# All two-tile attention groups of batches 2 to 4 turned by DMA transpose, and a list planner's durations replaced by measured ones

## The chip, the cores and the metric

The kernel runs on one core of one Trainium2 chip. The metric is the device time of one execution in microseconds (us). A core has five engines with an instruction queue each: PE (matmul), DVE (vector), ACT (activation), POOL (GpSimd) and SP, which here only issues DMAs. Each engine issues its own queue in order.

## The reference

Three layers follow one another, all in float32:

```
scores = q @ k^T / 8                          # 4 batches, 8 heads, 576 x 576, head size 64
keep   = scores >= rowmax(scores) - tau       # tau = 0.02
p      = softmax(scores where keep else -1e9)
x      = (p @ v), heads joined                # 2304 tokens x 512
y      = square(relu(x @ w_in)) @ w_out       # 512 -> 2048 -> 512
logits = y @ phi                              # 32 slots
slot_in  = softmax over tokens(logits)^T @ y
slot_out = relu(slot_in @ w1[e]) @ w2[e]      # 8 experts, 4 slots each
out    = softmax over slots(logits) @ slot_out
```

The second layer's weights arrive as float64 and are converted on the chip.

## The kernel before, in words

**Work.** A *pair* is two heads of one batch: 4 pairs per batch, 16 in all. A pair has five query tiles: four of 128 rows by both heads (in the code `j` 0 to 3), made into two *groups* (`g` 0 and 1) of two tiles, and one mixed tile of the last 64 rows of both heads (`g` 2). One tile is: scores on PE (`s_mm`, L471 to L482, one PSUM buffer); per head on DVE the clipped negative scores with their row extreme (`top`, L498), on POOL the bound extreme + tau (`bound`, L504), on ACT the exponential (`expo`, L510), on DVE the masking with its row sum (`keep`, L514).

**Two ways to turn the probabilities.** For the product with V they are needed transposed. *PE path*: nine 128x128 transposes per tile (`turn`, through the helper at L241), copied out of PSUM by ACT (`evac`, L579 and L577), then a float32 product with V (`av`, L627 and L616). *DMA path*: ACT makes a half-precision copy (`high`, L532), POOL the rest e - high, also in half precision (`low`, L536), both into a tile `hl` (two buffers), which SP turns with one DMA transpose (`dturn`, L543); then `av_split` (L635, L640) multiplies high by the high and low halves of V and low by the high half. The halves of V are made once per pair by `split_v` (into the only buffer `vh`), in every pair that has a group on this path. `by_dma(p, g)` decides: batch 1 and all mixed tiles go by PE; of batches 2 to 4 the second group of every pair, and the first group of the second and fourth pair. After either, row sums are inverted (`recip`, L599), spread, turned and multiplied in (`evac`, L657 or L659) into `xp`.

**Feed-forward.** Tokens go in nine units of 256 (two per batch, one of all remainders). A unit splits x into two parts (`xhi` L897, `xlo` L903), runs 16 blocks of 12 matmuls (`mm_half`, L932; the plan's `f_a` and `f_b`), squares on ACT and DVE, and then does the softmax step over slots and the accumulation of the slot inputs (`post`). A unit of a batch can only start when the batch's attention is done. The weight conversion (`conv_ops`) must be done before the first unit. `weights` and `tail` load w1 and w2 into buffers freed by attention and by the last unit, and finish.

**Order.** Nothing is ordered by hand. Every step is handed to `Plan` (`add`) with its engine, a modelled duration, its inputs, buffers it takes and gives back, and a key. `Plan.run` plays a clock: a free engine starts, among the steps whose inputs are ready and whose buffers are free, that of the lowest key, and emits its instructions then. That fixes each engine's queue for good; on the chip an instruction waits its turn even if a later one could run. Attention has low keys; feed-forward on PE has keys from 1e5 up, so that it fills what attention leaves. `LEAD` shifts keys by kind. A DMA is modelled on one bus: it starts 1.13 us after issue or when the bus is free, takes its `dma` time, and is seen 0.95 us after; a negative `dma` (the transpose) also holds SP until 0.95 us before the bus is free. SP issues nothing when the bus is booked more than 2.212 us ahead.

Of the kernel before, what the change touches and what calls it, by code (L numbers as in the profile page):

```python
# [139 lines left out]
def tile_kernel(  # L140
# [115 lines left out]
    def conv_ops():  # L256
# [10 lines left out]
        def chunk(n, w, r0, c0):  # L267
# [41 lines left out]
            a = add("c_scale", "ACT", 0.53, scale, [l], k, ["cv"])  # L309
            t = add("c_low", on, 0.53 if on == "ACT" else 0.35, low, [l], k)  # L310
            s = add("c_shift", "DVE", 0.61, shift, [a, t], k)
            if flip:
                s = [s, add("c_unit", "ACT", 0.53, unit, [a], k)]
                s = add("c_flip", "POOL", 1.25, sign, s, k, rel=[("raw64", l)])
            else:
                s = add("c_sign", "DVE", 0.61, sign, [s], k, rel=[("raw64", l)])
            if w is w_in:
                hi, lo = [w_sb[x, c0 // CW][:, r0 // 128, :] for x in ("h", "l")]
                h = add("c_hi", "ACT", 0.53, lambda: nc.scalar.activation(hi, o["p"], AF.Copy), [s], k)
                return add("c_lo", "POOL", 1.23, lambda: nc.gpsimd.tensor_tensor(lo, o["p"], hi.bitcast(F32), ALU.subtract),  # L320
                           [h], k, rel=[("cv", a)])
# [18 lines left out]
            g = add("c_turn", "PE", 0.6, turn, [s], k, ["mm", "wt"])  # L340
# [3 lines left out]
            pr = add("c_prod", "PE", 1.05, prod, [e, lphi], k, rel=[("wt", g)])  # L344
# [8 lines left out]
    def attn_ops():  # L353
# [56 lines left out]
        def split_v(x):  # L410
# [39 lines left out]
            sc = add("v_scale", "DVE", 0.5, scales, [st], k0, rel=[("mm", st)])  # L450
# [4 lines left out]
        def tiles(p):  # L455
# [5 lines left out]
            def tile_ops(n, j):  # L461
# [23 lines left out]
                S_ = add("s", "PE", 1.4, s_mm, d["ready"], k, ["s"])  # L485
# [3 lines left out]
                for a in heads:  # L489
# [92 lines left out]
                for x in heads + (2,):  # L582
# [3 lines left out]
                    t = add("turn", "PE", 0.13 if x == 2 else 0.49, lambda x=x: turn(x), dep + [gd.get("pto")], k, ["mm"] + new, [(tag, ee)])  # L586
                    v_ = add("p_evac", "ACT", 0.27 if x == 2 else 0.59, lambda x=x: evac(x), [t], k, [], [("mm", t)])
# [3 lines left out]
            def group_ops(g, n):  # L591
# [16 lines left out]
                rc = add("recip", "DVE", 0.5, recip, gd["keep"], k, ["rp"], [("sm", gd["first"])])  # L608
# [52 lines left out]
                if g < 2:  # L661
                    rc = add("spread", "POOL", 0.6, spread, [rc], k, ["rb"], [("rp", rc)])
# [13 lines left out]
                rt = add("r_turn", "PE", 0.13 if g == 2 else 0.26, rturn, [rc], k, ["mm", "rr"], rel)  # L676
                rc = add("r_evac", "ACT", 0.3 if g == 2 else 0.4, revac, [rt], k, [], [("mm", rt)])
                deps = gd["turn"] + [d["v_op"], d["vr_op"]]
                first = None
                if by_dma(p, g):  # L680
                    o = first = add("av", "PE", 1.9, av_split, deps + [d["vs_ready"]], k, ["ma"],
                                    [("pt", gd["pto"]), ("vh", d["vs_op"])])
                for lo, hi_ in () if by_dma(p, g) else ((0, 5),) if g == 2 else ((0, 2), (2, 5)):
                    c = (hi_ - lo) * (0.51 if g < 2 else 0.3) 
# [7 lines left out]
                ev = add("evac", "DVE", 0.25 if g == 2 else 0.45, evac, [o, rc], k, ["xp"] if g < 2 and kk == 0 else [], rel)  # L692
# [34 lines left out]
    def ffn_ops(units):  # L727
# [9 lines left out]
        def post(u, d, first, last):  # L737
# [77 lines left out]
            a0 = add("f_pl", "PE", 1.53, lambda: pl(0, MC // NG - 1), d["sq"][:-2], pk(), ["mm"])  # L815
            a = add("f_pm", "PE", 0.51, lambda: pl(MC // NG - 1, MC // NG), [a0] + d["sq"][-2:], pk())
            a2 = add("f_l4", "ACT", 0.26, lambda: nc.scalar.activation(l4, w["pl"][:, :NU], AF.Copy), [a], HI, ["l4"], [("mm", a0)])
            b_ = add("f_p12", "PE", 0.43, p12, [a2], pk(), ["mm"])
            bk = add("f_p1k", "PE", 0.35, p1k, [b_], pk(), [], [("l4", a2)])
            c = add("f_max", "DVE", 0.45, rowmax, [b_, fo.get("nm")], HI)  # L820
            e = add("f_alpha", "ACT", 0.5, alpha, [c, fo.get("nm")], HI, ["dT"], [("mm", b_)])
            f = add("f_total", "DVE", 0.12, total, [e, fo.get("ss")], HI)
            g = add("f_cmax", "DVE", 0.39, cmax, [bk], HI + 1)
            h = add("f_ce", "ACT", 0.15, lambda: nc.scalar.activation(w["ce"], w["ce"], AF.Exp), [g], HI + 1)
            add("f_csum", "DVE", 0.80, csum, [h], HI + 1, rel=[("mm", b_)])
            i_ = add("f_p3", "PE", 0.25, p3, [e], pk(), ["mm"], [("dT", e)])
            j_ = add("f_dk", "DVE", 0.2, dkc, [i_], HI, rel=[("mm", i_)])
            lastsg, turns = fo.get("sg"), []
            for t in range(T):
                gks, ro = [], []  # L830
                for j in range(NG):
# [23 lines left out]
                    ro.append(add("f_gk", "DVE" if dv else "ACT", 0.6 if dv else 0.49, evac, [tt], HI + 2, rel=[("mm", tt)]))  # L855
# [21 lines left out]
                for t_, (accum, merge, ro, gks) in enumerate(turns):  # L877
                    joint = last and t_
                    ac = add("f_acc", "PE", 0.93, accum, ro + [j_] + ([ac0] if joint else []), pk(), [] if joint else ["mm"], gks)
# [8 lines left out]
        for n, u in enumerate(units):  # L888
# [17 lines left out]
            for kk in range(KC):  # L906
# [3 lines left out]
                l = add("xlo", "DVE" if dv else "POOL", 0.35 if dv else 0.69, lambda f=xlo, kk=kk: f(kk), [h] + ls[:1],  # L910
# [332 lines left out]
```

## Time and profile before

| | us |
|---|---|
| three runs, lowest, median, highest | 695.98, 696.82, 704.65 |
| profiled execution, first to last instruction (span) | 694.8 |
| PE busy | 630.1 |
| DVE busy | 456.8 |
| ACT busy | 393.2 |
| POOL busy | 233.1 |

The page gives the profiled execution no time beside its span. Busy times are sums over the whole run, which has stages with different limits: weight conversion with batch 1 (to 155.7 us), attention of batches 2 to 4 with feed-forward units between (to 523.2 us), feed-forward alone (to 618.2 us), and the experts with the output. "PEld" is the loading of PE's stationary operand, "PEclk" the granted clock of TensorE as a share of its full speed.

### The profile page before, as it was taken

How to read it: one execution, taken by the hardware profiler on the slowest of the kernel's cores; microseconds unless marked ns; L12 is line 12 of the kernel's file. 1: busy time of each engine (PE TensorE's matmuls, PEld its weight loads, DVE VectorE, ACT ScalarE, POOL GpSimd, SP SyncE). 2: the span in 40 equal slices, each digit the busy share in tenths (PEclk: the TensorE clock that was granted, in tenths of full speed). 3: DMA queues.
4: the chain of work that ended last, by engine and by line, in shares of the span. 5: the costliest groups of instructions: out<-in, count | busy, mean ns of one | idle time of the engine just before them, and what ended most of it. 6: DMA issues, size and time to landing. Idle time of an engine off the chain costs nothing.

```text
span 694.8 us, 13413 instructions
## 1 busy us (share of the span) xinstructions
PE 630.1 (91%) x5084; PEld 458.4 (66%) x5084; DVE 456.8 (66%) x1183; ACT 393.2 (57%) x762; POOL 233.1 (34%) x308
## 2 busy tenths in 40 slices
PE   1566988999999999999999999999999999998883
PEld 0333656677857686677778667877788989883321
DVE  6999998975787868777966797778733132222503
ACT  4776756766765764766667557757653333331203
POOL 4866433212643434354244344344440000000000
PEclk9987999999999999999999999999999999999998
DMA  6854676422633545163437235352533940397987
GB/s 230 296 180 150 202 246 220 147 93 52 122 70 87 122 70 116 40 135 66 91 73 117 56 69 123 69 122 53 86 59 119 401 174 31 124 371 267 388 321 272
DMA packets 123056, 104.74 MB, mean 151 GB/s; under 512 B 90736, under 2 KB 95856, under 8 KB 122992
## 3 DMA queue, kind: packets, MB, share of 16 engines
q1 hardware_dynamic: 122992, 103.89, 52.0%
q8 instruction: 40, 0.66, 0.4%
q14 instruction: 24, 0.20, 0.1%
HBM read 73.73 MB, written 8.91 MB: 119 GB/s over the span
## 4 chain that ended last, share of the span: by engine, by line
PE 74%; DVE 10%; DMA 5%; ACT 4%; issue 4%; POOL 1%; SPq 0%; DVEq 0%; POOLq 0%; ACTq 0%
PE mm L932 30%; PE mm L241 11%; PE s L482 8%; PE po L627 4%; DVE e L514 3%; PE po L635 3%; PE mm L861 2%; PE mm L747 2%; PE mm L1063 2%; DMA w<-in_moe_w_dram 2%; PE s L477 2%; DMA w_out<-cv 2%; PE s L471 2%; DVE cv L293 2%; ACT e L510 1%
## 5 line engine op out<-in xcount | busy, mean ns | idle before, releaser
L932 PE MATMUL mm<-xh,w 128*128 128x256 f32 x1152 | 167.1, 288 | 0.0
L932 PEld LDWEIGHTS mm<-xh,w 128*128 128x128 f32 x1152 | 147.4, 191 | 16.7 <-issue 10.5
L514 DVE SCALAR_TENSOR_TENSOR e<-u,sm,e 128x576 f32<-128x576 f32 x144 | 125.4, 885 | 26.1 <-ACT e L510 22.9
L498 DVE TENSOR_SCALAR_CACHE_REDUCE u<-s,nscale 128x576 f32<-128x576 f32 x144 | 115.3, 811 | 26.0 <-PE s L482 20.5
L510 ACT ACTIVATE e<-u,sm 128x576 f32<-128x576 f32 x144 | 109.3, 775 | 38.7 <-DVE u L498 36.4
L536 POOL TENSOR_TENSOR hl<-e,hl 128x576 f16<-128x576 f32 x72 | 95.5, 1337 | 84.6 <-ACT hl L532 69.9
L504 POOL TENSOR_SCALAR sm<-sm,tau_p 128x1 f32<-128x1 f32 x144 | 60.7, 424 | 141.1 <-DVE u L498 108.9
L932 PE MATMUL mm<-xl,w 128*128 128x256 f32 x576 | 92.4, 283 | 0.0
L938 ACT ACTIVATE gt<-mm 128x512 f32<-128x512 f32 x72 | 42.9, 596 | 83.3 <-PE mm L932 82.8
L932 PEld LDWEIGHTS mm<-xl,w 128*128 128x128 f32 x576 | 79.3, 192 | 0.0
L482 PE MATMUL s<-kt,qt 64*128 64x512 f32 x256 | 77.0, 680 | 0.0
L241 PE MATMUL mm<-ident_r,e 128*128 128x128 f32 (+1 forms) x332 | 53.3, 296 | 6.0 <-DVE e L514 5.2
L241 PEld LDWEIGHTS mm<-ident_r,e 128*128 128x128 f32 (+1 forms) x332 | 39.9, 151 | 26.8 <-issue 10.0
L477 PE MATMUL s<-kt,qt 128*128 128x128 f32 x128 | 27.2, 295 | 31.0 <-DMA qt<-in_q_dram 11.8
L532 ACT ACTIVATE hl<-e 128x576 f16<-128x576 f32 x72 | 48.1, 679 | 11.8 <-DVE e L514 11.5
L579 ACT ACTIVATE pt<-mm 128x512 f32<-128x512 f32 x72 | 41.7, 594 | 21.9 <-PE mm L241 21.6
L944 DVE SCALAR_TENSOR_TENSOR gt<-mm,gt 128x512 f32<-128x512 f32 x18 | 12.4, 690 | 61.1 <-ACT gt L938 60.3
L477 PEld LDWEIGHTS s<-kt,qt 128*128 128x128 f32 x128 | 20.8, 199 | 36.1 <-issue 19.7
L627 PE MATMUL po<-pt,raw 128*64 128x64 f32 (+1 forms) x480 | 42.0, 309 | 0.0
L241 PE MATMUL mm<-ident_r,gt 128*128 128x128 f32 x288 | 38.3, 278 | 1.4 <-DVE ar L813 1.4
L241 PEld LDWEIGHTS mm<-ident_r,gt 128*128 128x128 f32 x288 | 31.5, 142 | 12.1 <-issue 8.2
L946 ACT ACTIVATE gt<-gt 128x512 f32<-128x512 f32 x54 | 33.9, 627 | 1.1
(148 smaller groups left out, 889.4 us busy)
## 6 DMA issues: line engine op xcount, KB each, us to landing
w<-in_moe_w_dram SPq DMA_DIRECT2D x25, 1024.0 KB, 11.9
raw<-in_moe_w_in_dram SPq DMA_DIRECT2D x16, 512.0 KB, 4.3
raw<-in_moe_w_out_dram SPq DMA_DIRECT2D x16, 512.0 KB, 4.0
kt<-in_k_dram SPq DMA_DIRECT2D x20, 320.0 KB, 3.3
qt<-in_q_dram SPq DMA_DIRECT2D x20, 320.0 KB, 3.7
raw<-in_v_dram SPq DMA_DIRECT2D x20, 256.0 KB, 3.1
w_out<-cv SPq DMA_DIRECT2D x16, 256.0 KB, 4.7
w<-w_out SPq DMA_DIRECT2D x4, 1024.0 KB, 9.1
```

The costliest lines, as they stand in the source:

```text
L241: nc.tensor.transpose(out_, in_, ident[:n, :n])
L477: nc.tensor.matmul(s[:, 1].rearrange("p (c s) -> p c s", s=64)[:, 0:8:7], lt, d["kt"][:, 512:SQ], start=True, stop=True)
L482: nc.tensor.matmul(s[:, 2 * a], lt[i], d["kt"][i, 0:512], start=True, stop=True)
L498: nc.vector.tensor_scalar(u, o["s"][:, s0:s0 + S], nscale, None, ALU.mult, ALU.min, accum_out=gd["sm"][:, c:c + 1])
L504: nc.gpsimd.tensor_scalar(sm[:, 4 + c:5 + c], sm[:, c:c + 1], tau_p, None, ALU.add)
L510: nc.scalar.activation(e, o["u", a], AF.Exp, scale=-1.0, bias=gd["sm"][:, c:c + 1])
L514: nc.vector.scalar_tensor_tensor(e, o["u", a], sm[:, 4 + c:5 + c], e, ALU.is_le, ALU.mult, accum_out=sm[:, 8 + c:9 + c])
L532: nc.scalar.activation(o["hl"][:, a * S:(a + 1) * S], o["e"][:, a * S:(a + 1) * S], AF.Copy)
L536: nc.gpsimd.tensor_tensor(o["hl"][:, (2 + a) * S:(3 + a) * S], o["e"][:, c], o["hl"][:, c], ALU.subtract)
L627: nc.tensor.matmul(po[i, :n_], lt, rh, start=m == 0, stop=m == 4)
L932: nc.tensor.matmul(o["h"][:, i * NU:(i + 1) * NU], a, c, start=n_ == 0, stop=n_ == len(terms) - 1)
L938: nc.scalar.activation(g, o["h"], AF.Relu)
```

## The change

`by_dma` now sends every two-tile group of batches 2 to 4 to the DMA path, 24 groups where there were 18. And the modelled durations of about thirty kinds of steps are set to other values. No instruction of any other step is changed; its place in its queue may be.

```diff
         def by_dma(p, g):
             b, n = jobs[p][0] // NP, jobs[p][0] % NP
-            return g < 2 and (b > 0 and (g == 1 or n % 2 == 1))
+            return g < 2 and b > 0
...
-            g = add("c_turn", "PE", 0.6, turn, [s], k, ["mm", "wt"])
+            g = add("c_turn", "PE", 0.47, turn, [s], k, ["mm", "wt"])
...
-                S_ = add("s", "PE", 1.4, s_mm, d["ready"], k, ["s"])
+                S_ = add("s", "PE", 1.28 if mixed else 1.38, s_mm, d["ready"], k, ["s"])
...
-                    X = add("top", "DVE", 0.89, top, [S_], k, ["u"] + (["sm"] if first_g and not a else []), [("s", S_)])
+                    X = add("top", "DVE", 0.75, top, [S_], k, ["u"] + (["sm"] if first_g and not a else []), [("s", S_)])
...
-                    h = add("bound", "POOL", 0.52, bound, [X], k)
-                    E_ = add("expo", "ACT", 0.77, expo, [X] + ([ee] if a else []), k, [] if a else ["e"])
+                    h = add("bound", "POOL", 0.26, bound, [X], k)
+                    E_ = add("expo", "ACT", 0.67, expo, [X] + ([ee] if a else []), k, [] if a else ["e"])
...
-                    K_ = add("keep", "DVE", 0.92, keep, [E_, h], k, rel=[("u", X)])
+                    K_ = add("keep", "DVE", 0.75, keep, [E_, h], k, rel=[("u", X)])
...
-                        h = add("high", "ACT", 0.68, lambda a=a: high(a), [ks[a]] + ([hl] if a else []), k, [] if a else ["hl"])
+                        h = add("high", "ACT", 0.58, lambda a=a: high(a), [ks[a]] + ([hl] if a else []), k, [] if a else ["hl"])
...
-                        ls.append(add("low", "POOL", 1.72, lambda a=a: low(a), [h], k, rel=[("e", ee)]))
+                        ls.append(add("low", "POOL", 1.28, lambda a=a: low(a), [h], k, rel=[("e", ee)]))
...
-                    t = add("dturn", "SP", 3.0, dturn, ls, k, [] if "pto" in gd else ["pt"], [("hl", hl)], dma=-6.8)
+                    t = add("dturn", "SP", 2.75, dturn, ls, k, [] if "pto" in gd else ["pt"], [("hl", hl)], dma=-3.2)
...
-                    o = first = add("av", "PE", 1.9, av_split, deps + [d["vs_ready"]], k, ["ma"],
+                    o = first = add("av", "PE", 1.83, av_split, deps + [d["vs_ready"]], k, ["ma"],
...
-                a = add("f_a", "PE", 1.31, lambda f=mm_half: f(0), hs + ls + ms[-1:] + (conv if n == 0 else []), pk(), ["mm", "gt"])
-                b_ = add("f_b", "PE", 1.31, lambda f=mm_half: f(1), [a], pk())
+                a = add("f_a", "PE", 1.44, lambda f=mm_half: f(0), hs + ls + ms[-1:] + (conv if n == 0 else []), pk(), ["mm", "gt"])
+                b_ = add("f_b", "PE", 1.44, lambda f=mm_half: f(1), [a], pk())
```

The rest of the diff changes durations in the same manner: of the conversion (`c_scale` 0.53 to 0.57, `c_lo` 1.23 to 1.4, `c_prod` 1.05 to 0.93 and others), of `turn`, `p_evac`, `recip`, `spread`, `r_turn`, `r_evac`, the PE path's `av` and `evac`, of `xlo`, and of the steps of `post` (most by less than 0.15).

## Rows read from the trace of the kernel before

**Rows 1.** The page's busy table: engine, busy us, share of span, instructions.
```profile
PE 630.1 (91%) x5084; PEld 458.4 (66%) x5084; DVE 456.8 (66%) x1183; ACT 393.2 (57%) x762; POOL 233.1 (34%) x308
```

**Rows 2.** The table by stage; its first line names the columns.
```profile
core 0: us, PE busy (x) PEld busy (x) DVE busy (x) ACT busy (x) POOL busy (x), PEclk, DMA share, GB/s
0.00:155.70 155.70, 116.47 (x745) 76.11 (x746) 137.18 (x313) 103.91 (x195) 74.57 (x89) 0.93 0.60 196
155.70:523.20 367.50, 361.47 (x3079) 273.60 (x3077) 271.84 (x752) 239.34 (x474) 153.71 (x213) 1.00 0.43 86
523.20:618.20 95.00, 94.37 (x816) 84.50 (x815) 23.27 (x55) 33.64 (x62) 3.02 (x5) 1.00 0.50 194
618.20:694.80 76.60, 57.76 (x451) 24.17 (x449) 24.51 (x66) 16.33 (x33) 1.79 (x2) 0.94 0.84 317
```

**Rows 3.** The chain of waits from 155.7 to 523.2 us, shares by line.
```profile
by line: PE mm L932 38.5%; PE s L482 12.4%; PE mm L241 11.9%; PE po L627 5.2%; PE po L635 5.1%; DVE e L514 3.2%; PE s L477 2.9%; PE mm L747 2.7%; PE mm L861 2.5%; PE s L471 2.4%; PE po L640 1.5%; issue 1.2%; PE mm L424 1.1%; PE po L616 0.9%
```

**Rows 4.** Pieces of the chain in the last two stages: start us, us, what.
```profile
532.11 20.34 PE mm L932 x168
...
656.10 13.41 DMA w<-in_moe_w_dram
```

**Rows 5.** Pieces of the chain, a group on the PE path, 285 to 297 us.
```profile
290.04 1.73 PE mm L241 x14
...
294.26 1.88 PE po L627 x16
296.14 0.63 PE po L616 x2
```

**Rows 6.** Pieces of the chain, a product on the DMA path, 285 to 297 us.
```profile
285.97 1.43 PE po L635 x24
287.40 0.43 PE po L640 x3
```

**Rows 7.** By line, 155.7 to 523.2 us: count, ns min/median/max, first and last start.
```profile
L532 ACT ACTIVATE hl<-e x72: 666/676/716, 163.5 to 514.8; 128x576 f16<-128x576 f32 x72
...
L536 POOL TENSOR_TENSOR hl<-e,hl x72: 1269/1287/1872, 164.3 to 516.6; 128x576 f16<-128x576 f32 x72
...
L579 ACT ACTIVATE pt<-mm x36: 578/598/617, 155.5 to 518.2; 128x512 f32<-128x512 f32 x36
...
L577 ACT ACTIVATE pt<-mm x24: 250/267/309, 156.5 to 518.7; 128x128 f32<-128x128 f32 x12, 64x128 f32<-64x128 f32 x12
...
L543 SPq DMA_TRANSPOSE pt<-hl x36: 2457/2705/3585, 168.7 to 517.9; - x36
...
DMA to landing us min/median/max: 4.5/4.6/6.3
```

**Rows 8.** By line, the same columns and stretch, three lines of DVE.
```profile
L514 DVE SCALAR_TENSOR_TENSOR e<-u,sm,e x106: 799/816/1921, 156.2 to 506.9; 128x576 f32<-128x576 f32 x106
...
L599 DVE TENSOR_SCALAR sm<-sm x36: 122/163/1245, 160.1 to 507.8; 128x4 f32<-128x4 f32 x24, 128x1 f32<-128x1 f32 x12
...
L897 DVE CAST xh<-xp x23: 273/290/1371, 196.7 to 518.8; 128x256 fp32r<-128x256 f32 x23
```

**Rows 9.** Groups of DVE instructions, 155.7 to 523.2 us: busy us, mean ns, idle before.
```profile
L514 DVE SCALAR_TENSOR_TENSOR e<-u,sm,e 128x576 f32<-128x576 f32 x106 | 89.1, 856 | 22.1 <-ACT e L510 19.4 <-POOL sm L504 2.2 <-issue 0.4
...
L599 DVE TENSOR_SCALAR sm<-sm 128x4 f32<-128x4 f32 (+1 forms) x36 | 11.5, 319 | 0.3
L897 DVE CAST xh<-xp 128x256 fp32r<-128x256 f32 x23 | 9.9, 438 | 1.6 <-PE mm L932 1.5
```

**Rows 10.** Pieces of the chain around the end of batch 3, 385 to 406 us.
```profile
385.00 2.05 PE mm L932 x17
...
389.01 1.94 DVE e L514 x2
...
390.97 1.13 DVE sm L599
...
405.41 0.60 PE mm L932 x5
```

More of the change, by code (lines that the diff above doesn't have):

```diff
@@ L308, in chunk @@
             l = add("c_load", "SP", 0.5, load, key=k - 8, acq=["raw64"], dma=1.46)
-            a = add("c_scale", "ACT", 0.53, scale, [l], k, ["cv"])
-            t = add("c_low", on, 0.53 if on == "ACT" else 0.35, low, [l], k)
+            a = add("c_scale", "ACT", 0.57, scale, [l], k, ["cv"])
+            t = add("c_low", on, 0.57 if on == "ACT" else 0.34, low, [l], k)
             s = add("c_shift", "DVE", 0.61, shift, [a, t], k)
             if flip:
-                s = [s, add("c_unit", "ACT", 0.53, unit, [a], k)]
-                s = add("c_flip", "POOL", 1.25, sign, s, k, rel=[("raw64", l)])
+                s = [s, add("c_unit", "ACT", 0.57, unit, [a], k)]
+                s = add("c_flip", "POOL", 1.31, sign, s, k, rel=[("raw64", l)])
             else:
@@ L319, in chunk @@
                 h = add("c_hi", "ACT", 0.53, lambda: nc.scalar.activation(hi, o["p"], AF.Copy), [s], k)
-                return add("c_lo", "POOL", 1.23, lambda: nc.gpsimd.tensor_tensor(lo, o["p"], hi.bitcast(F32), ALU.subtract),
+                return add("c_lo", "POOL", 1.4, lambda: nc.gpsimd.tensor_tensor(lo, o["p"], hi.bitcast(F32), ALU.subtract),
                            [h], k, rel=[("cv", a)])
@@ L449, in split_v @@
             st = add("v_sum", "PE", 0.4, stats, [ab], k0, ["mm"])
-            sc = add("v_scale", "DVE", 0.5, scales, [st], k0, rel=[("mm", st)])
+            sc = add("v_scale", "DVE", 0.45, scales, [st], k0, rel=[("mm", st)])
             h = add("v_hi", "ACT", 0.9, hi, [sc], k0)
@@ L585, in tile_ops @@
                     new = [] if "pto" in gd else [pk]
-                    t = add("turn", "PE", 0.13 if x == 2 else 0.49, lambda x=x: turn(x), dep + [gd.get("pto")], k, ["mm"] + new, [(tag, ee)])
-                    v_ = add("p_evac", "ACT", 0.27 if x == 2 else 0.59, lambda x=x: evac(x), [t], k, [], [("mm", t)])
+                    t = add("turn", "PE", 0.12 if x == 2 else 0.45, lambda x=x: turn(x), dep + [gd.get("pto")], k, ["mm"] + new, [(tag, ee)])
+                    v_ = add("p_evac", "ACT", 0.17 if x == 2 else 0.49, lambda x=x: evac(x), [t], k, [], [("mm", t)])
                     gd.setdefault("pto", t)
@@ L606, in spread @@
                     nc.gpsimd.tensor_copy(gd["rb"].rearrange("p (t a d) -> p t a d", t=2, a=2), y)
-                rc = add("recip", "DVE", 0.5, recip, gd["keep"], k, ["rp"], [("sm", gd["first"])])
+                rc = add("recip", "DVE", 0.32, recip, gd["keep"], k, ["rp"], [("sm", gd["first"])])
                 def av(lo, hi):
@@ L661, in group_ops @@
                 if g < 2:
-                    rc = add("spread", "POOL", 0.6, spread, [rc], k, ["rb"], [("rp", rc)])
+                    rc = add("spread", "POOL", 0.38, spread, [rc], k, ["rb"], [("rp", rc)])
                 def rturn():
@@ L675, in group_ops @@
                 rel = [("rp" if g == 2 else "rb", rc)]
-                rt = add("r_turn", "PE", 0.13 if g == 2 else 0.26, rturn, [rc], k, ["mm", "rr"], rel)
-                rc = add("r_evac", "ACT", 0.3 if g == 2 else 0.4, revac, [rt], k, [], [("mm", rt)])
+                rt = add("r_turn", "PE", 0.12 if g == 2 else 0.23, rturn, [rc], k, ["mm", "rr"], rel)
+                rc = add("r_evac", "ACT", 0.17 if g == 2 else 0.27, revac, [rt], k, [], [("mm", rt)])
                 deps = gd["turn"] + [d["v_op"], d["vr_op"]]
@@ L691, in group_ops @@
                 rel = [("ma", first), ("rr", rt)] + ([("mx", d["vs_op"])] if by_dma(p, g) else [])
-                ev = add("evac", "DVE", 0.25 if g == 2 else 0.45, evac, [o, rc], k, ["xp"] if g < 2 and kk == 0 else [], rel)
+                ev = add("evac", "DVE", 0.42 if g == 2 else 0.4, evac, [o, rc], k, ["xp"] if g < 2 and kk == 0 else [], rel)
                 ev_at.setdefault("rem" if g == 2 else (b, g), []).append(ev)
@@ L854, in post @@
                     dv = j in GKD
-                    ro.append(add("f_gk", "DVE" if dv else "ACT", 0.6 if dv else 0.49, evac, [tt], HI + 2, rel=[("mm", tt)]))
+                    ro.append(add("f_gk", "DVE" if dv else "ACT", 0.6 if dv else 0.48, evac, [tt], HI + 2, rel=[("mm", tt)]))
                 def accum(t=t):
@@ L909, in ffn_ops @@
                 dv = kk in SPH
-                l = add("xlo", "DVE" if dv else "POOL", 0.35 if dv else 0.69, lambda f=xlo, kk=kk: f(kk), [h] + ls[:1],
+                l = add("xlo", "DVE" if dv else "POOL", 0.34 if dv else 0.71, lambda f=xlo, kk=kk: f(kk), [h] + ls[:1],
                         HI, [] if kk else ["xl"], [] if u == "rem" else [("xp", xdeps[0])])
```

24 lines of the change are left out of this document (12 added, 12 removed).

## Prediction

> **What bounds the kernel now.** I read the busy table first: TensorE (PE) is busy for 630 of the 694.8 us [rows 1]. That is an average, so the table by stage comes next [rows 2]. To 155.7 us (weight conversion, batch 1) VectorE (DVE) is the full engine, 137.2 of 155.7. From there to 523.2 us (attention of batches 2 to 4 with six feed-forward units as filling) PE is busy 361.5 of 367.5 us, DVE 272, ACT 239, POOL 154. To 618.2 us three more units run alone, PE 94.4 of 95.0. The last 76.6 us wait on weight loads as well.
>
> A busy PE may be a waiting one, since ends of matmuls are modelled. So the third view is the chain of waits in the middle stretch [rows 3]: its twelve PE lines sum to 87.1% there; DVE, "issue" and lines too short to be listed share the other 12.9%, 47 us. PE's own work sets the pace of this stretch, and some 30 us of it (an estimate, between nothing and those 47) are waits on others. What is taken off PE there shortens the run, if nothing new is waited for.
>
> The three units alone go at 20.34/168 = 0.121 us per matmul, and the end has a 13.4 us wait for a weight load [rows 4]. Those loads go into buffers that the last unit frees, so the last two stretches move with the middle one and keep their lengths.
>
> **The change, part by part.** (1) Six groups of two tiles (the first group of the first and third pair, three batches by two) leave the PE path: 18 of 24 groups were turned by DMA (36 transposes), all 24 will be (48).
>
> PE work removed, per group: 18 transposes at 1.73/14 = 0.124 us, 2.22 us, and the product with V, 1.88 + 0.63 = 2.51 us [rows 5]. Added: the split product, 1.43 + 0.43 = 1.86 us [rows 6]. Net 2.22 + 2.51 - 1.86 = 2.87 us, times six **17.2 us**. All these rows are pieces of the chain, so I take them off in full.
>
> ACT, per group: four wide evictions (0.598) and two narrow ones (0.267) go, 2.93 us; four half-precision copies at 0.676 come, 2.70 us [rows 7]. Over six groups -1.3 us, at no effect: ACT is 65% busy there.
>
> POOL: 24 subtractions of 1.287 us more [rows 7], 30.9 us. POOL goes from 154 to 185 us of some 350, so it has time. But it runs in order, and the 0.3 us `bound` that the next `keep` needs now stands behind a subtraction more often. Bound: nothing to 1.29 each.
>
> SP queue: 12 transposes at 2.705 us, 32.5 us of issuing, in a queue that also issues the q, k and v loads; a transpose waiting for POOL holds the loads behind it. They are issued a pair ahead, and a pair takes 367.5/12 = 30.6 us, so I cost it at nothing; without that cover one late load costs PE the 4.6 us that a landing takes. The DMA engines are 43% busy [rows 2].
>
> V is already split for every pair of batches 2 to 4, so nothing is added there, but in the first and third pair the split is needed two tiles earlier.
>
> (2) The price that only overlap shows is on DVE. `keep` (L514) has a median of 0.816 us and a maximum of 1.921 us [rows 8], and a mean of 0.856 us [rows 9]: 106 x 0.04 = 4.2 us above the median. The small add of `recip` (L599) has 0.163 and 0.319 us, 36 x 0.156 = 5.6 us; the cast `xhi` (L897) 0.290 and 0.438 us, 23 x 0.148 = 3.4 us. Charged wholly to the 72 subtractions on POOL (an attribution, not shown) these 13.2 us are 0.183 us each; 24 more give 4.4 us of DVE time. Lower end nothing (DVE is 74% busy in this stretch); upper end the whole subtraction on the path, 24 x 1.29 = 31 us. I take a quarter of the 4.4, **+1.1 us**, near the lower end, because the rows with the mean lie there.
>
> The Trainium skill (SBUF — State Buffer, "Who interferes with whom") speaks against the change here: a DVE instruction with two SBUF inputs, or a copy or cast in a two-port mode, and a GpSimd instruction that reads SBUF hold one port pair exclusively, and the loser is blocked for the whole instruction. The 1.921 us maximum agrees, the mean does not show it as the rule of most cases; by the full block the sum would be +31 us.
>
> (3) The modelled durations only reorder. The large one is the DMA turn: in the plan it held SP for 1.13 + 6.8 - 0.95 = 6.98 us and landed after 8.88; now 1.13 + 3.2 - 0.95 = 3.38, and 5.28. The trace has 4.5/4.6/6.3 us to landing [rows 7]. `top`, `keep`, `bound` and `low` shrink towards the measured pitches, `f_a`/`f_b` grow by a tenth, to 12 x 0.12 = 1.44. Two effects oppose. Four turns took 28 us of SP in a 30.6 us pair of the old plan, so the plan itself kept attention slow, and feed-forward ran dry: between 387.05 and 405.41 no matmul of L932 stands in the chain, and DVE pieces do [rows 10], 1.94 us of `keep` and 1.13 of the add the longest of them. With 13.5 us per pair attention can run ahead and leave PE a stock of filling. On the other hand the old margins vanish: `av` was placed 4.3 us after the usual landing, now 0.7 us, and the longest landing seen is 1.0 us beyond it. PE issues in order, so behind a late `av` stand the next scores and all the filling, and behind the scores DVE. Bounds: -12 us (`keep` 1.94, the add 1.13 and some 0.9 of smaller DVE pieces, 4 us, at the ends of three batches) to 24 groups x 1.0 = +24. I take nothing for the middle.
>
> (4) Before 155.7 us nothing moves to another engine. The idle 155.7 - 137.2 = 18.5 us of DVE [rows 2], the fullest engine there, bound a gain; a reorder could as well cost one weight chunk's wait, some 6 us (estimate from the 4.6 us landing and the 1.3 us operations behind it). Taken as nothing.
>
> **Sum.** 694.8 - 17.2 + 1.1 = 678.7 us of span. The page gives no time of its own for the profiled execution beyond its span; the median run is 2.0 us above it, so 680.7: **681 us**, 2.3% faster.
>
> **Rivals.**
> *The plan gains too.* Attention runs ahead, PE never lacks filling, and the 12 us at the batch ends go as well: 681 - 12 = 669. For it: the 18.4 us without L932. Against: the key offsets of the plan stay as set for the old durations, and real overlap costs are still not in the model.
>
> *New waits eat half or all.* PE waits for a transpose or a `keep` at the 24 groups, 0.35 to 0.7 us each: +8 to +17, so 689 to 697. For it: margin 0.7 against a spread of 1.7 us in landings. Against: filling blocks of 1.44 us that cannot be interrupted put most attention work on PE later than its inputs.
>
> *Slower, by the port.* Each of the 24 new subtractions blocks `keep` for its length, and `keep` leads to scores and to `high`, so it comes onto the path: 679.6 + 31 = 711. It decides from 17.2/24 = 0.72 us of path per subtraction. For it: the 1.94 us pair of `keep` in the chain [rows 10]. Against: 0.183 us on average now. This is also what the port rule of the Trainium skill gives if every one collides.
>
> That the change does nothing can be excluded: the condition leaves no two-tile group of batches 2 to 4 on the PE path.
>
> **Chances.** Forecast, 676 to 686: 0.50. Plan gains: 0.17. Half or all eaten: 0.22. Slower than before: 0.11, of it 0.05 beyond 2% (above 710.8). Two per cent, 13.9 us, is about what timings of this kernel tell from no change. Faster by that is below 682.9: the second case whole and two thirds of the first, 0.50; slower 0.05; within, 0.45. The range, 667 to 696, holds the forecast, nearly all of the second and third cases, and leaves out the fourth and the far ends.
>
> **What would show it.** In the profile after: 48 transposes, 96 half-precision copies and 96 subtractions; 108 fewer transposes of `e` on PE; the middle stretch near 351 us with PE still at 98%, the other three unchanged within 3 us. If the plan gains, no gap in L932 as long as 18 us until attention ends, and attention ends well before the sixth unit. If waits eat it, PE or its weight loads wait for `pt` or `s` by name, and the chain's DVE and DMA share rises. If the port decides, `keep` has a mean well over 0.86 us. The forecast is wrong if PE's work falls by 17 us and the stretch does not.

## The result, and the profile after

The changed kernel takes 704.31 us (median of 20 runs, 699.18 to 706.59) where the kernel before takes 698.99 us (median of 20, 695.82 to 704.65). The ratio is 1.0073, with a 95% interval of 1.0052 to 1.0094: slower by 0.7%, well within 2% but clear of noise. The forecast was 681 us and a range of 667 to 696. The profiled execution has a span of 704.5 us and took 706.3. Two single runs in a slower state, one of the kernel before (708.7 us) and one of a kernel below (713.4 us), are left out of the times here.

Two things about the numbers to be compared. The traces differ by 9.7 us of span (694.8 and 704.5) where the medians differ by 5.3: the trace of before is of one of its faster runs. And the three runs that the forecast started from have a median of 696.82 us, 2.2 below that of the twenty.

The first view is the busy table of the page after the change. Under it is the page's chain by engine, first after the change, then before.

```profile
PE 631.9 (90%) x5030; PEld 457.7 (65%) x5030; DVE 465.1 (66%) x1183; ACT 393.5 (56%) x750; POOL 261.6 (37%) x332
```

```profile
PE 55%; DVE 18%; ACT 8%; DMA 6%; POOL 6%; issue 5%; SPq 1%; DVEq 0%; ACTq 0%; POOLq 0%
```

```profile
PE 74%; DVE 10%; DMA 5%; ACT 4%; issue 4%; POOL 1%; SPq 0%; DVEq 0%; POOLq 0%; ACTq 0%
```

PE is busy for the same time as before [rows 1], although its work has shrunk. The chain tells why that number misleads: PE has 55% of it, where it had 74%; DVE rose from 10% to 18%, ACT from 4% to 8% and POOL from 1% to 6%.

The table by stage, cut at the first feed-forward matmul, at the last eviction of attention and at the last feed-forward matmul, answers to [rows 2].

```profile
core 0: us, PE busy (x) PEld busy (x) DVE busy (x) ACT busy (x) POOL busy (x), PEclk, DMA share, GB/s
0.00:154.00 154.00, 119.22 (x723) 78.86 (x723) 134.74 (x305) 101.43 (x192) 73.36 (x90) 0.91 0.60 198
154.00:485.80 331.80, 314.45 (x2652) 229.06 (x2652) 268.88 (x717) 223.60 (x428) 180.50 (x232) 0.96 0.58 116
485.80:627.70 141.90, 140.45 (x1212) 125.61 (x1210) 37.00 (x97) 52.11 (x98) 5.94 (x9) 1.00 0.35 130
627.70:704.50 76.80, 57.77 (x451) 24.17 (x449) 24.48 (x66) 16.33 (x33) 1.80 (x2) 0.94 0.84 316
```

Conversion took 154.0 us (155.7 before), the last stage 76.8 (76.6). The change is between them. Attention ended at 485.8 us instead of 531.2 (the last eviction; the 523.2 of [rows 2] stands 8 us before it), so it did run ahead, but the nine feed-forward units ended at 627.7 instead of 618.2: from the first to the last of them 473.7 us where it was 462.5. The clock column fell from 1.00 to 0.96 in the stretch of attention.

The work went as written in the diff. These are groups of the whole run: line, count, busy us, mean ns. The first two rows are of the changed kernel, the last two of the kernel before.

```profile
L241 PE MATMUL mm<-ident_r,e 128*128 128x128 f32 (+1 forms) x224 | 39.2, 310 | 7.0 <-DVE e L514 6.8 <-ACT pt L579 0.2
L635 PE MATMUL po<-pt,vh 128*64 128x256 f16 x576 | 35.9, 274 | 2.5 <-DVE xr L648 2.5
```

```profile
L241 PE MATMUL mm<-ident_r,e 128*128 128x128 f32 (+1 forms) x332 | 53.3, 296 | 6.0 <-DVE e L514 5.2 <-DVE wphi L345 0.7
L635 PE MATMUL po<-pt,vh 128*64 128x256 f16 x432 | 27.0, 275 | 0.0
```

224 transposes of `e` instead of 332, 576 products with the split V instead of 432. To see what this is worth, I add up PE's work between the first and last feed-forward matmul as counts times the undisturbed distance from start to start that the trace of before has for each kind (0.12 us for L932, and so on): 439.9 us before, 424.6 after. That is 15 us less, near the 17.2 of the forecast. The stretch is 11.2 us longer, so PE waits some 26 us more: 49 us instead of 23. (The sums are estimates of mine from the starts in the two traces. With the mean distance of each kind where PE did not wait they are 441 and 423, so they carry an error of some 3 us.)

Where it waits is in the chain of the stretch of attention, to be read against [rows 3], and in the waits of DVE and PE there (engine, line waited for: us in total, times, longest).

```profile
by line: PE mm L932 18.4%; PE s L482 9.3%; POOL hl L536 7.7%; DVE e L514 6.9%; issue 6.1%; PE mm L241 6.0%; PE po L635 4.2%; DVE u L498 3.7%; PE s L477 3.1%; ACT e L510 3.0%; PE mm L861 2.7%; DVE xh L897 2.2%; ACT hl L532 2.2%; POOL sm L504
```

```profile
DVE e L514 <- POOL sm L504: 21.8, 23, 1.9
...
PEld mm L241 <- POOL sm L504: 4.7, 5, 1.7
...
PE s L477 <- DVE u L498: 3.6, 7, 1.2
```

POOL's subtraction `low` (L536) is on the chain with 7.7% of 331.8 us, 26 us; before it was not in the list. `keep` waited 21.8 us for `bound` on POOL where the trace of before has 2.2. How it gets there is seen in the pieces of the chain at 291 us (start, us, what).

```profile
291.38 0.69 ACT hl L532
...
292.14 1.28 POOL hl L536
293.42 0.27 POOL sm L504
...
293.72 0.83 DVE e L514 x2
```

An ACT copy releases a subtraction of 1.28 us; `bound`, 0.27 us, stands behind it in POOL's queue; `keep` needs `bound`. Nothing of the four pieces is PE's. PE itself ran scores at that time and one more block of feed-forward to 295.5 us.

About half of what PE lost lies in what its queue holds after such a block. By the starts of L932's matmuls, the changed kernel has four stretches above 18 us, before attention ends, without one of them: 20.6 us from 215.3, 25.8 from 295.5, 26.1 from 375.6 and 19.2 from 430.9. The kernel before has two, of 18.4 and 18.1. Two of the four in the table by stage, cut where no matmul of L932 is left:

```profile
core 0: us, PE busy (x) PEld busy (x) DVE busy (x) ACT busy (x) POOL busy (x), PEclk, DMA share, GB/s
295.70:321.20 25.50, 22.82 (x192) 12.11 (x192) 23.26 (x64) 17.17 (x37) 13.26 (x19) 0.93 0.57 119
375.80:401.50 25.70, 22.82 (x193) 12.54 (x191) 22.98 (x63) 17.32 (x37) 13.25 (x19) 0.93 0.58 118
```

DVE is 91% and 89% busy there, and PE has attention and the steps of `post` alone. By the sums above, with mean distances, the four stretches hold some 24 us of what PE lost (an estimate). Three of them lie inside a unit that had already run its first blocks, so feed-forward was left to do, and it stands later in PE's queue. Whether its buffers would have let it run earlier no run shows.

Three lines of DVE answer to [rows 9], and the transposes to [rows 7].

```profile
L514 DVE SCALAR_TENSOR_TENSOR e<-u,sm,e 128x576 f32<-128x576 f32 x107 | 90.8, 861 | 35.0 <-POOL sm L504 21.8 <-ACT e L510 12.3
...
L599 DVE TENSOR_SCALAR sm<-sm 128x4 f32<-128x4 f32 (+1 forms) x36 | 18.7, 520 | 0.1
...
L897 DVE CAST xh<-xp 128x256 fp32r<-128x256 f32 x17 | 10.1, 621 | 1.0 <-PE mm L932 1.0
```

```profile
L543 SPq DMA_TRANSPOSE pt<-hl x48: 2414/2706/4134, 160.2 to 476.9; - x48
...
DMA to landing us min/median/max: 4.5/4.6/6.4
```

`keep` has a mean of 0.861 us (0.856 before): no slower in the mean. The add of `recip` went from 0.319 to 0.520 us and the casts from 0.438 to 0.621. The transposes land as before, 4.6 us in the median and 6.4 at most.

### The profile page after: what moved, and what is told of

Its sections match the earlier page's. It is cut to its first block, busy times and chain, and to the rows that moved or that the text cites. A ratio compares the mean times of both kernels' runs of the same rounds, so it can differ in the third digit from the quotient of the medians.

```text
span 704.5 us, 13387 instructions
## 1 busy us (share of the span) xinstructions
PE 631.9 (90%) x5030; PEld 457.7 (65%) x5030; DVE 465.1 (66%) x1183; ACT 393.5 (56%) x750; POOL 261.6 (37%) x332
## 4 chain that ended last, share of the span: by engine, by line
PE 55%; DVE 18%; ACT 8%; DMA 6%; POOL 6%; issue 5%; SPq 1%; DVEq 0%; ACTq 0%; POOLq 0%
PE mm L932 23%; PE mm L241 8%; PE s L482 5%; DVE e L514 4%; POOL hl L536 4%; PE mm L861 3%; DVE u L498 3%; PE po L627 2%; ACT e L510 2%; DMA w_out<-cv 2%; PE mm L1063 2%; PE po L635 2%; DMA w<-in_moe_w_dram 2%; PE mm L747 2%; PE s L477 2%
## 5 line engine op out<-in xcount | busy, mean ns | idle before, releaser
L932 PE MATMUL mm<-xh,w 128*128 128x256 f32 x1152 | 167.3, 288 | 0.0
L536 POOL TENSOR_TENSOR hl<-e,hl 128x576 f16<-128x576 f32 x96 | 128.0, 1346 | 87.3 <-ACT hl L532 79.6
L932 PEld LDWEIGHTS mm<-xh,w 128*128 128x128 f32 x1152 | 147.7, 191 | 17.0 <-issue 12.5
L932 PE MATMUL mm<-xl,w 128*128 128x256 f32 x576 | 92.4, 283 | 0.0
L504 POOL TENSOR_SCALAR sm<-sm,tau_p 128x1 f32<-128x1 f32 x144 | 53.2, 374 | 87.7 <-DVE u L498 64.4
L482 PE MATMUL s<-kt,qt 64*128 64x512 f32 x256 | 81.4, 715 | 0.0
L932 PEld LDWEIGHTS mm<-xl,w 128*128 128x128 f32 x576 | 79.4, 192 | 0.0
L532 ACT ACTIVATE hl<-e 128x576 f16<-128x576 f32 x96 | 64.6, 678 | 25.5 <-DVE e L514 24.2
L477 PE MATMUL s<-kt,qt 128*128 128x128 f32 x128 | 30.6, 324 | 29.4 <-DMA qt<-in_q_dram 12.6
L903 POOL TENSOR_TENSOR xl<-xp,xh 128x256 fp32r<-128x256 f32 x16 | 13.6, 862 | 86.4 <-PE mm L932 84.6
L241 PE MATMUL mm<-ident_r,e 128*128 128x128 f32 (+1 forms) x224 | 39.2, 310 | 7.0 <-DVE e L514 6.8
L241 PEld LDWEIGHTS mm<-ident_r,e 128*128 128x128 f32 (+1 forms) x224 | 28.6, 156 | 23.5 <-DVE e L514 9.0
L579 ACT ACTIVATE pt<-mm 128x512 f32<-128x512 f32 x48 | 28.4, 598 | 24.7 <-PE mm L241 22.0
L635 PE MATMUL po<-pt,vh 128*64 128x256 f16 x576 | 35.9, 274 | 2.5 <-DVE xr L648 2.5
## 6 DMA issues: line engine op xcount, KB each, us to landing
w<-in_moe_w_dram SPq DMA_DIRECT2D x25, 1024.0 KB, 12.2
```

Source lines behind the costliest of these rows:

```text
L241: nc.tensor.transpose(out_, in_, ident[:n, :n])
L477: nc.tensor.matmul(s[:, 1].rearrange("p (c s) -> p c s", s=64)[:, 0:8:7], lt, d["kt"][:, 512:SQ], start=True, stop=True)
L482: nc.tensor.matmul(s[:, 2 * a], lt[i], d["kt"][i, 0:512], start=True, stop=True)
L504: nc.gpsimd.tensor_scalar(sm[:, 4 + c:5 + c], sm[:, c:c + 1], tau_p, None, ALU.add)
L532: nc.scalar.activation(o["hl"][:, a * S:(a + 1) * S], o["e"][:, a * S:(a + 1) * S], AF.Copy)
L536: nc.gpsimd.tensor_tensor(o["hl"][:, (2 + a) * S:(3 + a) * S], o["e"][:, c], o["hl"][:, c], ALU.subtract)
```

## The experiments

Each was timed beside the kernel before on the same chip; ratios are to it, with 95% intervals. Theory M: the new durations took away margins, and PE meets late inputs. Theory G: the six groups themselves cost it. Later ones are named where they come up.

### The two halves of the change

Groups alone: `by_dma` as changed, everything else as before. Durations alone: the reverse.

```diff
-            return g < 2 and (b > 0 and (g == 1 or n % 2 == 1))
+            return g < 2 and b > 0
```

> All 24 groups by DMA transpose, every modelled duration as before. Theory M (the new durations took the margins away, and PE's fixed order now meets inputs that are late): the groups alone give what was forecast for them, 12 to 17 us less, ratio to the kernel before 0.975 to 0.983. Theory G (the six more groups themselves cost it, by the port and by POOL's order): no gain or a loss, ratio 1.00 to 1.02.

> The 18 groups of before, all modelled durations new. Theory M: the loss is here, the waits of the changed kernel (26 us more than before) without the 17 us of PE work saved, ratio 1.02 to 1.04. Theory G: close to the kernel before, 0.99 to 1.01.

Measured: groups alone 716.07 us, ratio 1.0264 [1.0198, 1.0330]; durations alone 707.34 us, 1.0126 [1.0081, 1.0170]. Both halves lose, the groups clearly more than the two together (1.0073); the interval of the durations overlaps that of the two. Theory M as I had put it fell with the groups alone, which should have been fast. Neither theory has an interaction of this sign: new durations make the kernel slower with 18 groups and faster with 24.

In the groups alone attention ended at 557.8 us, 27 us later than before, and between units there were stretches of 27.9, 41.7 and 37.5 us without a feed-forward matmul. That pointed to the plan's DMA turn: at 6.98 us of SP each, the plan lets a pair with four of them pass no faster than one in 28 us, and now every pair has four. Call it theory S: the long modelled turn holds attention back until feed-forward has nothing left to fill with.

### Seven attention durations put back, then six

The first kernel is the changed one with `top`, `bound`, `expo`, `keep`, `high`, `low` and `dturn` at their old values. The second leaves `dturn` at its new one and has this edit; the first has it and the line of `dturn` (3.0 and -6.8) as well:

```diff
-                    X = add("top", "DVE", 0.75, top, [S_], k, ["u"] + (["sm"] if first_g and not a else []), [("s", S_)])
+                    X = add("top", "DVE", 0.89, top, [S_], k, ["u"] + (["sm"] if first_g and not a else []), [("s", S_)])
...
-                    h = add("bound", "POOL", 0.26, bound, [X], k)
+                    h = add("bound", "POOL", 0.52, bound, [X], k)
...
-                    E_ = add("expo", "ACT", 0.67, expo, [X] + ([ee] if a else []), k, [] if a else ["e"])
+                    E_ = add("expo", "ACT", 0.77, expo, [X] + ([ee] if a else []), k, [] if a else ["e"])
...
-                    K_ = add("keep", "DVE", 0.75, keep, [E_, h], k, rel=[("u", X)])
+                    K_ = add("keep", "DVE", 0.92, keep, [E_, h], k, rel=[("u", X)])
...
-                        h = add("high", "ACT", 0.58, lambda a=a: high(a), [ks[a]] + ([hl] if a else []), k, [] if a else ["hl"])
+                        h = add("high", "ACT", 0.68, lambda a=a: high(a), [ks[a]] + ([hl] if a else []), k, [] if a else ["hl"])
...
-                        ls.append(add("low", "POOL", 1.28, lambda a=a: low(a), [h], k, rel=[("e", ee)]))
+                        ls.append(add("low", "POOL", 1.72, lambda a=a: low(a), [h], k, rel=[("e", ee)]))
```

> The changed kernel with the modelled durations of seven attention steps (top, bound, expo, keep, high, low, dturn) put back to those of before; all others new. Theory M: most of the 26 us of added waits go, about 682 us, ratio 0.97 to 0.985, close to the groups alone. Theory G: stays near 704 us, ratio 1.00 to 1.01.

> The changed kernel with six attention durations (top, bound, expo, keep, high, low) put back to the longer ones of before, and the new short one of the DMA turn kept. Theory S with M (the old turn of 7 us made the groups alone slow, since attention is held back and feed-forward runs dry; the new short chain makes PE meet late inputs): both faults are absent, 680 to 692 us, ratio 0.975 to 0.99, attention's end between 490 and 530 us. Theory L: 703 to 718 us.

Measured: seven back 715.63 us, 1.0234 [1.0184, 1.0284]; six back 685.06 us, 0.9801 [0.9734, 0.9868]. Seven back is no other than the groups alone (716.07), so with 24 groups the rest of the changed durations is worth nothing to be seen: these seven carry it all. The two kernels here differ in `dturn` alone, 3.0 and -6.8 against 2.75 and -3.2, and that is worth 30.6 us. The view that shows it is the busy time of the feed-forward line (L932) alone, in four neighbouring stretches of the kernel with seven back.

```profile
core 0: us, PE busy (x) PEld busy (x), PEclk, DMA share, GB/s
321.10:375.80 54.70, 24.99 (x192) 23.42 (x192) 0.97 0.46 94
375.80:419.30 43.50, 0.30 (x4) 0.09 (x2) 0.84 0.43 86
...
502.00:547.60 45.60, 7.94 (x60) 7.34 (x60) 0.93 0.41 69
```

A unit runs to 375.8 us, and for the next 43.5 us there are four matmuls of L932 (the next unit's batch is not through attention), with the clock at 0.84; before 547.6 us the same again. Theory S holds. The kernel with six back has no stretch without feed-forward above 18 us before attention ends:

```profile
core 0: us, PE busy (x) PEld busy (x) DVE busy (x) ACT busy (x) POOL busy (x), PEclk, DMA share, GB/s
0.00:151.30 151.30, 117.60 (x736) 76.91 (x736) 135.99 (x308) 102.95 (x194) 77.14 (x89) 0.93 0.62 202
151.30:502.10 350.80, 339.81 (x2970) 258.07 (x2967) 278.54 (x738) 236.53 (x452) 187.26 (x236) 1.00 0.56 110
502.10:605.20 103.10, 102.06 (x882) 90.92 (x881) 27.62 (x72) 37.54 (x71) 4.45 (x7) 1.00 0.48 179
605.20:681.70 76.50, 57.79 (x451) 24.26 (x449) 24.50 (x66) 16.32 (x33) 1.80 (x2) 0.93 0.85 317
```

```profile
by line: PE mm L932 34.2%; PE s L482 12.1%; PE po L635 8.5%; PE mm L241 7.9%; PE s L477 3.5%; DVE u L498 3.1%; DVE e L514 2.9%; PE po L627 2.8%; issue 2.7%; PE po L640 2.6%; PE s L471 2.6%; PE mm L861 2.6%; DVE xh L897 1.5%; DVE vh L446 1.5
```

Attention ends at 502.1, between the two extremes, the clock column is back at 1.00, L932 has 34% of the chain (18.4% in the changed kernel), and `low` and `bound` are not among the listed lines. The first to the last feed-forward matmul take 453.8 us: 15 us less work than before and some 6 us more of waits. This kernel beats both, by 2.0% and 2.7%.

### What the groups are worth under a sound plan

The same durations with the 18 groups of before.

```diff
-            return g < 2 and b > 0
+            return g < 2 and (b > 0 and (g == 1 or n % 2 == 1))
```

> The plan's durations as in the best kernel so far (685 us: the changed kernel with the six longer attention durations), but 18 groups by DMA as before. The price of the six groups alone under an order without either fault: if the 17 us of PE work are worth their sum, 698 to 704 us, ratio 1.00 to 1.01; if the gain of that kernel came from the order alone, 683 to 690 us.

Measured: 700.96 us, 1.0021 [0.9991, 1.0050]. Against 685.06 the six groups give 15.9 us, where the sum of the prediction had 17.2 - 1.1 = 16.1. The two intervals leave some 5 us either way, so the sum is borne out, and that the figures agree to 0.2 is luck. Under the durations of the changed kernel the same groups give 3 us (707.34 against 704.31), and under the old ones they cost 18 (716.07 against 698.22, the kernel before beside it).

### Is it the lengths, or a lucky order

Theory L: the key offsets were fitted to the old durations, and any other set gives a worse order. Two kernels nudge one constant of the plan by 0.01 us.

```diff
-HOP = 0.17
+HOP = 0.18
```

> The kernel before with HOP 0.18 instead of 0.17 us: no work and no duration of a step is changed, only the plan's order where near ties fall the other way. Theory L: the fitted order is lost, 703 to 718 us, ratio 1.01 to 1.03. Theory M and theory S (a slow modelled DMA turn holds attention back): an equivalent order, 695 to 702 us, ratio 0.995 to 1.005.

> The changed kernel with HOP 0.18 instead of 0.17 us. Theory L: another draw of an order that is not fitted, anywhere from 695 to 718 us. Theory M: the margin is hardly changed, 700 to 708 us.

Measured: before with the nudge 701.35 us, 1.0009 [0.9981, 1.0037]; after with it 704.54 us, 1.0082 [1.0048, 1.0116]. Other orders, same times. Theory L falls, at least for differences of 1% and more, by one other order of each kernel. The kernel with six back was not nudged; that its nearest relatives below take 688.53 and 690.31 us speaks against luck.

A third kernel raises the constant to 0.40 on the changed one: later inputs at each hand-over, the same busy times.

```diff
-HOP = 0.17
+HOP = 0.40
```

> The changed kernel with one constant of the plan raised: the time from one engine's end to another engine's start, HOP, 0.17 to 0.40 us, so that every input is modelled as later by 0.23 us per hand-over and all busy times stay as they are. Theory M (late inputs stall PE since the margins are gone): waits of PE in the stretch with feed-forward fall from 49 us towards the 23 us of before, 680 to 692 us, ratio 0.975 to 0.99. Theory L (the key offsets were fitted to the one set of durations of before, and any other set gives a worse order): 700 to 718 us, no trend with margin.

Measured: 704.72 us, 1.0068 [1.0036, 1.0101]. No gain, though in its profiled run (699.8 us, the fastest) `keep` waited only 12.2 us for `bound`; three stretches of 23 to 26 us without feed-forward were left. So it is not the time between engines that the plan lacked. What helped in the kernel with six back are longer busy times, which also slow the pace at which the plan feeds attention to the engines.

### Which lengths

The changed kernel with old durations of DVE alone (`top`, `keep`), of POOL alone (`bound`, `low`), of ACT alone (`expo`, `high`), and of DVE and POOL together; and the kernel with six back with DVE's and POOL's raised further. The edits are the lines named from the diff above; the last one is:

```diff
-                    X = add("top", "DVE", 0.89, top, [S_], k, ["u"] + (["sm"] if first_g and not a else []), [("s", S_)])
+                    X = add("top", "DVE", 1.00, top, [S_], k, ["u"] + (["sm"] if first_g and not a else []), [("s", S_)])
...
-                    h = add("bound", "POOL", 0.52, bound, [X], k)
+                    h = add("bound", "POOL", 0.60, bound, [X], k)
...
-                    K_ = add("keep", "DVE", 0.92, keep, [E_, h], k, rel=[("u", X)])
+                    K_ = add("keep", "DVE", 1.05, keep, [E_, h], k, rel=[("u", X)])
...
-                        ls.append(add("low", "POOL", 1.72, lambda a=a: low(a), [h], k, rel=[("e", ee)]))
+                        ls.append(add("low", "POOL", 2.00, lambda a=a: low(a), [h], k, rel=[("e", ee)]))
```

> The changed kernel with the two DVE durations alone put back (top 0.89, keep 0.92). Theory D (the plan packs DVE tighter than DVE runs, so it puts too little feed-forward between two attention steps on PE): most of what the six durations gave, 682 to 692 us, ratio 0.975 to 0.99. Theory P (the lateness is POOL's: bound and low take longer than modelled and keep waits for bound): 698 to 708 us, ratio 1.00 to 1.01.

> The changed kernel with the two POOL durations alone put back (bound 0.52, low 1.72). Theory P: 682 to 692 us, and keep's waits for bound fall from 22 us to under 8. Theory D: 698 to 708 us.

> The changed kernel with the two ACT durations alone put back (expo 0.77, high 0.68). ACT is the least loaded of the three, so both theories D and P expect no gain: 699 to 708 us, ratio 1.00 to 1.01. If any longer attention chain would do, by whatever engine, 685 to 695 us.

> The changed kernel with the DVE and the POOL durations put back together (top, keep, bound, low), ACT's as changed. If the two lengths make up all of the 19 us that the six gave, since ACT's alone gave nothing: 683 to 688 us, ratio 0.977 to 0.985. If ACT's lengths matter beside the others: 690 to 697 us.

> The best kernel so far with its DVE and POOL lengths raised further (top 1.00, keep 1.05, bound 0.60, low 2.00). If room in the plan is what PE lacked and more of it is still better: 675 to 683 us. If the lengths are about right and more of them holds attention back, as the old DMA turn did: 688 to 705 us, with longer stretches without feed-forward matmuls before attention ends.

| kernel | us | ratio to before | 95% |
|---|---|---|---|
| changed | 704.31 | 1.0073 | 1.0052 to 1.0094 |
| DVE's two back | 694.76 | 0.9925 | 0.9894 to 0.9955 |
| POOL's two back | 690.31 | 0.9868 | 0.9798 to 0.9939 |
| ACT's two back | 703.17 | 1.0057 | 1.0024 to 1.0090 |
| DVE's and POOL's back | 688.53 | 0.9857 | 0.9830 to 0.9883 |
| all six back | 685.06 | 0.9801 | 0.9734 to 0.9868 |
| raised further | 701.36 | 1.0036 | 1.0005 to 1.0068 |

POOL's two give 14 us, DVE's two 10, both together hardly more than POOL's; ACT's alone nothing. Of all six against four, 3.5 us, the intervals overlap, so ACT's part stays open; `bound` and `low` were not put back apart. DVE's two came out between the ranges of both theories, POOL's two in that of theory P. `keep`'s waits for `bound` look like the mechanism, and are not the whole of it. The first row is of the kernel with POOL's two back, the second of that with DVE's, the third of that with ACT's.

```profile
DVE e L514 <- POOL sm L504: 2.3, 6, 0.8
```

```profile
DVE e L514 <- POOL sm L504: 21.7, 27, 2.0
```

```profile
DVE e L514 <- POOL sm L504: 10.7, 15, 1.4
```

With POOL's lengths the 21.8 us of the changed kernel go to 2.3, as before the change. With DVE's they stay at 21.7, and the kernel is still 10 us faster. With ACT's they are halved, and the kernel is no faster. Its chain of attention no longer lists `low` (L536) at all, which in the changed kernel stood on 26 us of it:

```profile
by line: PE mm L932 28.7%; PE s L482 11.7%; PE po L635 7.9%; PE mm L241 6.5%; DVE e L514 4.9%; DMA pt<-hl 3.4%; PE s L477 3.2%; issue 2.7%; DVE u L498 2.6%; PE mm L861 2.5%; PE po L640 2.3%; PE po L627 2.3%; PE mm L747 2.2%; PE s L471 2.1%;
```

So POOL's queue is where the changed kernel waited in this run, and not by itself what sets the time. Among the kernels with 24 groups and the new turn, the time goes better with the filling. Stretches above 18 us without a matmul of L932 before attention ends: none in the kernels with six and with POOL's two back, one (20.4 us) with DVE's and POOL's, two (22.4 and 21.8) with DVE's, three with ACT's (23.9, 22.1, 19.6) and four in the changed kernel. This is a count over one trace each, not a test by itself, and with 18 groups it does not order the kernels (two with the durations alone, 707 us, and three with the six lengths back, 701 us). Raised further, attention ended at 541.4 us and stretches of 25 to 27 us without feed-forward were back. Of the sets tried, the old lengths of the six are the best; the shorter and the longer ones both leave PE stretches without filling.

### `bound` moved to DVE

```diff
-                        nc.gpsimd.tensor_scalar(sm[:, 4 + c:5 + c], sm[:, c:c + 1], tau_p, None, ALU.add)
+                        nc.vector.tensor_scalar(sm[:, 4 + c:5 + c], sm[:, c:c + 1], tau_p, None, ALU.add)
...
-                    h = add("bound", "POOL", 0.26, bound, [X], k)
+                    h = add("bound", "DVE", 0.15, bound, [X], k)
```

> The changed kernel with the small step bound (128x1) issued on DVE instead of POOL, modelled at 0.15 us. If what is late is keep behind a bound that stands behind subtractions in POOL's queue (22 us of such DVE waits in the changed kernel, 2 before), a good part of the 26 us goes: 685 to 692, ratio 0.98 to 0.99. If the lateness is general (DMA, ACT and DVE alike), it stays within 5 us of the changed kernel, ratio 1.00 to 1.01.

Measured: 717.77 us, 1.0285 [1.0237, 1.0334]. It takes `bound` out of POOL's queue and is 13 us slower than the changed kernel: 144 more instructions on DVE, at about 0.2 us each in its trace, lengthen the engine that attention uses most (268.9 of 331.8 us in the changed kernel's stretch). Whether the wait behind POOL's subtractions or the added DVE work weighs more it cannot tell, since it changes both.

## Why the prediction was wrong

**What bounds the kernel: right, under one plan.** PE's own work paced it before, and taking the groups off PE gives 15.9 us with the six old lengths and the new turn (18 against 24 groups). Under the two other plans that were run it gives 3 us or loses 18.

**Work removed (part 1): right,** 17.2 forecast, 15 to 18 counted in the trace after, 15.9 measured under that plan.

**SP at nothing: right. ACT at nothing: right for its busy time only.** No transpose landed later than 6.4 us, and no PE wait in the changed kernel names one (`DMA pt<-hl`). ACT's busy time is the same (393.5 after 393.2 us), but its share of the page's chain doubled to 8%.

**POOL at nothing to 1.29 each, taken as nothing: the wait came, its price stays open.** I had named the step, `bound` behind a subtraction, and then given it no price, since POOL has time. It is 54% busy in the stretch (180.5 of 331.8 us) and its subtractions stand on 26 us of the chain. But those 26 us are not by themselves the loss: with ACT's two lengths back `low` is no longer among the chain's listed lines, and the time is the same.

**The port (part 2), +1.1 us: mechanism seen, size small.** Against the medians of [rows 8] DVE lost 107 x 0.045 + 36 x 0.357 + 17 x 0.331 = 23 us in the changed kernel, 13.2 before: 10 us more of DVE time instead of 4.4. The traces bear out the cause for the small steps: in the changed kernel the 24 adds of `recip` that overlap a subtraction on POOL took 0.78 us in the median, the 12 others 0.15. What part of the 10 us lies on the path no run separates. `keep`'s mean stayed at 0.86 us, so the rival "slower, by the port" fails by its own sign, and the full block that the Trainium skill states (SBUF — State Buffer, "Who interferes with whom") is not what most `keep`s show: the 28 of 107 that overlap a subtraction have the median of the others, 0.82 us, and 7 of them took over 0.9.

**The modelled durations (part 3), "I take nothing for the middle": this is the step that failed.** I had two opposite effects and let them cancel. Both are real and larger than I had them, and they come from different durations. The shorter attention steps cost 19 us (704.3 against 685.1); with those six lengths left as they were, the rest of the forecast holds (685.1 against 681). The shorter DMA turn is worth 30.6 us with 24 groups (I had allowed 12 for all of the gain), and the six groups could not be priced apart from it: under the old turn they cost 18 us in place of giving 16. I had read that brake into the kernel before, by four turns in every pair; there half of the pairs have two, on average three (36 in 12 pairs), 21 us of SP in 30.6. It is the six groups that make it four in every pair. The place of the new waits was wrong, too: I looked at the landing of transposes, where the margin was 0.7 us. No PE wait there names a landing; PE lost about half of its time in stretches without feed-forward, with DVE and POOL on the chain.

**The range.** The bound of part 3 was +24 us, and 681 + 24 = 705 is where the kernel landed; the range ended at 696, because the rival with new waits was cut at 17. A bound that is worked out belongs in the range. That the number fits is luck: the bound priced late landings of transposes, which did not come, and its base was 2 us low.

**Stages 1 and 4 unchanged within 3 us: right** (-1.7 and +0.2). The counts came true too (48 transposes, 96 subtractions, 108 fewer transposes of `e`). But the stretch of attention has PE at 95%, not 98%, the units alone take 141.9 us instead of 95.0, and the gaps in L932 grew from 18 to 26 us. "Attention ends well before the sixth unit" came true, at 485.8 us with the sixth unit's first matmul at 501, but I had tied it to a gain. The stock of filling that it left did not help: PE's queue had it behind the steps of attention, not between them.

## What to carry to other kernels

A planner's durations do two jobs, the length of the work and the pace at which work is released; here six durations set to the trace's busy times made the order 19 us worse, so change them one engine at a time and look where the filling went. Price a change of path together with the planner's model of the new path: the same six groups cost 18 us under one modelled DMA turn and give 16 under another. An engine's share of the chain in one trace says where that run waited, not what its removal is worth: POOL's 26 us went with another engine's lengths and nothing was gained.

## What the runs showed that I had not expected

PE lost clock where it waited. Before the change the granted clock is, in the run that was traced, 1.00 all through the stretch from 155.7 to 618.2 us; in the changed kernel it is 0.96 from 154.0 to 485.8, at most 0.04 x 331.8 = 13 us of PE time. One place, by the table by stage and by PE's instructions in order of time:

```profile
core 0: us, PE busy (x) PEld busy (x) DVE busy (x) ACT busy (x) POOL busy (x), PEclk, DMA share, GB/s
219.00:225.00 6.00, 4.57 (x47) 2.60 (x39) 5.55 (x16) 4.14 (x9) 3.33 (x5) 0.99 0.42 80
225.00:231.80 6.80, 6.69 (x25) 3.19 (x26) 5.29 (x20) 2.27 (x6) 1.92 (x4) 0.51 0.88 202
```

```profile
222.94 0.63 PE L760 MATMUL mm<-stack_f,l 128*128 128x32 f32 x4
225.11 0.42 PE L241 MATMUL mm<-ident_r,dT 32*128 32x32 f32 x2 [1.55 <-ACT dT L770]
225.46 0.80 PE L477 MATMUL s<-kt,qt 128*128 128x128 f32 x2
226.19 2.08 PE L482 MATMUL s<-kt,qt 64*128 64x512 f32 x4
```

PE started nothing between 222.94 + 0.63 and 225.11 us, then the clock was at 0.51 of 2.4 GHz, its lower level of 1.2, for 6.8 us, and the four score matmuls took 2.08 us where 1.13 is usual. If the wait brought the lower clock, it cost more than its length. Summed over the stretch, matmuls in such spells ran 10 us over their undisturbed times, of the 49 us that PE lost; that these spells follow from the waits was not tested by itself. The clock fell five times in the stretch of attention, and four of the five spells lie in the four stretches without feed-forward named above.

The kernel before varied from 695.4 to 704.8 us over its runs, and the time goes with the granted clock: 0.979 of full speed in the run of 695.7 us, 0.963 in that of 704.8. What lowers the clock in some runs and not in others I did not find out.
